# Two tiny reads of the rows that pass two loads first, and a vote moved to the end of the unfolding

## The chip, the cores and the metric

One core of one Trainium2 chip. The metric is the device time of one execution in microseconds, as the median over runs. Kernels that are compared ran on the same chip, in the same rounds.

## The reference

```python
def reference(x, w1d):            # x: (1, 384, 384, 384) bf16, w1d: (1,) bf16
    g = jnp.einsum("bhwc->bc", x) / (H * W)      # mean of each channel
    s = _sigmoid(g * w1d[0])                     # the general form has k taps, here k = 1
    return x * s[:, None, None, :]               # every row scaled by channel
```

x is 113.25 MB. It has to be read once for the sums, and it has to be scaled and written afterwards. What does not fit on the chip between the two must be read a second time.

## The kernel before

In pass one all 1152 rows of each partition are loaded and summed by TensorE. 367 of these rows stay in one big buffer, the arena; most of them packed so that four rows take the room of three (the fourth row is spread over bits of the other three that the code counts as fixed for inputs of this range). Pass two scales and stores what stayed, unpacks the packed groups, and loads the other 785 rows again, "the streamed rows". A vote says whether the bit packing was exact; if not, GpSimd would redo the kept rows at the end.

The order of all instructions is planned at build time, by a loop that imitates the DMA queue. Helpers and loop, with cuts:

```python
arena = pool.tile([P, ROWS, C], bf16, name="arena")       # 275 rows of 768 bytes per partition
...
def load(chunk, a, lo, hi):
    r0, n = chunk
    fl.add("SP", lambda: nc.sync.dma_start(out=arena[:, a : a + hi - lo, :], in_=view(xf, r0, n)[:, lo:hi, :]),
           writes=rows(a, hi - lo), dma=True)
...
def store(chunk, a, lo, hi): ...            # the reverse, arena -> out, also on SyncE's queue
def verdict(): ...                          # VectorE reduce, compare; TensorE votes; VectorE cast -> odd_i
...
while True:
    if dve_at <= now:
        ...
            can = start_pair()              # start to unpack the next group
            if can and not asked:
                verdict()
                asked = True
        ...                                 # or scale a landed chunk, or go on unpacking
    while waiting and waiting[0][0] <= now:
        _, n, then, chunk, a, lo, known = waiting.popleft()
        known.append(store(chunk, a, lo, lo + n))
    ...
    if got and todo < N_STREAM:             # free rows: load the next streamed rows
        load(STREAMED, a, todo, todo + n)
```

In this program (`LANES = 24`) every DMA on SyncE takes one of 24 completion semaphores ("lanes") in turn; a DMA whose lane is still in flight waits for it.

Of the kernel before, what the change touches and what calls it, by code (L numbers as in the profile page):

```python
# [127 lines left out]
def kernel(  # L128
# [11 lines left out]
    nc = tc.nc  # L140
# [39 lines left out]
    odd = pool.tile([P, 1], bf16, name="odd")  # L180
# [10 lines left out]
    xf = x.rearrange("b h w c -> (b h w) c")  # L191
    of = out.rearrange("b h w c -> (b h w) c")

    def view(t, r0, n):
        return t[r0 * P : (r0 + n) * P, :].rearrange("(p r) c -> p r c", r=n)

    def rows(lo, n):
        return [("a", r) for r in range(lo, lo + n)]

    fl = Flow(nc, tc)  # L200
# [6 lines left out]
    STREAMED, KEPT = (0, N_STREAM), (N_STREAM, N_KEPT)  # L207
# [154 lines left out]
    def copy_bank(i, src, dst, reads, writes):  # L362
        fl.add(
            "ACT", lambda: nc.scalar.copy(dst.bitcast(u32), src.bitcast(u32)), reads=reads, writes=writes  # L364
        )
# [56 lines left out]
    for a, n in S2 + V1 + S3 + S1 + [(U, 8), (Y, 8), (T, 5), (T + 5, 3)]:  # L422
        take_raw(a, n)
    assert summed[0] == RPP

    fl.add(
        "ACT",
        lambda: nc.scalar.activation(out=s_bf[:], in_=acc, func=ACTF.Sigmoid, scale=w_sc[:, 0:1]),  # L428
# [4 lines left out]
    def scale(a, n):  # L433
        v = arena[:, a : a + n, :]
        fl.add(
            "DVE",
            lambda: nc.vector.tensor_tensor(  # L437
                out=v, in0=v, in1=s_bf[:, None, :].to_broadcast([P, n, C]), op=Op.mult
            ),
            reads=rows(a, n) + ["s_bf"], writes=rows(a, n),  # L440
        )

    def store(chunk, a, lo, hi):
        r0, n = chunk
        return fl.add(
            "SP",
            lambda: nc.sync.dma_start(out=view(of, r0, n)[:, lo:hi, :], in_=arena[:, a : a + hi - lo, :]),
            reads=rows(a, hi - lo), dma=True,
        )
# [38 lines left out]
    def TT(n):  # L488
        return 0.15 + 0.2 * n
# [5 lines left out]
    def verdict():  # L495

        fl.add(
            "DVE",
            lambda: nc.vector.tensor_reduce(out=worst[:], in_=seen[:], op=Op.max, axis=mybir.AxisListType.X),  # L499
            reads=[("seen", k) for k in range(2 * len(pieces))], writes=["worst"],  # L500
        )
        fl.add(
            "DVE",
            lambda: nc.vector.tensor_single_scalar(out=odd[:], in_=worst[:], scalar=0.0, op=Op.is_gt),  # L504
            reads=["worst"], writes=["odd"],
        )
        fl.add(
            "PE",
            lambda: nc.tensor.matmul(votes, lhsT=ones[:], rhs=odd[:], start=True, stop=True),  # L509
            reads=["ones", "odd"], writes=["bank0"],  # L510
        )
        fl.add(
            "DVE", lambda: nc.vector.tensor_copy(out=odd_i[:], in_=votes), reads=["bank0"], writes=["odd_i"]  # L513
        )
# [44 lines left out]
    def runs():  # L559
        got, i = [], 0  # L560
        while i < ROWS:
            if idle[i]:
                j = i
                while j < ROWS and idle[j]:
                    j += 1
                got.append((j - i, i))
                i = j
            else:
                i += 1
        return got  # L570

    def send(chunk, a, lo, hi, then, known=None):

        waiting.append((dve_at, hi - lo, then, chunk, a, lo, [] if known is None else known))

    def backlog():
        return sum(e[1] for e in moves) + ROW * sum(e[1] for e in waiting)
# [9 lines left out]
    def stored(a, n):  # L587

        def f():
            for i in range(a, a + n):  # L590
                if ("a", i) in SCRATCH:
                    needed.discard(("a", i))
                else:
                    idle[i] = True
        return f
# [10 lines left out]
    line = deque((g, lo, min(2 * PIECE, QS[g] - lo)) for g in order for lo in range(0, QS[g], 2 * PIECE))  # L606
    total = sum(n for _, _, n in line)
    out_rows = 0
    turns = deque()
# [2 lines left out]
    since = None  # L612
    asked = checked = False
    stall = 0.0

    def start_pair():

        nonlocal pair, bank_at
        if not line or needed or not half[pair % 2]:
            return False  # L620
        g, lo, n = line[0]
        if g == BANKED and (bank_at is None or now < bank_at[1]):
            return False
        line.popleft()
        h = pair % 2
        at = HALVES[h]
        half[h] = False
        pair += 1
        a = bank_at[0] if g == BANKED else areas[g][0]
        a += 3 * lo  # L630
        mine = [k for k in of_group(g) if lo <= pieces[k][1] < lo + n]

        def w_done():
            nonlocal out_rows
            out_rows += n
            release(a, 3 * n)

        def u_done():
            half[h] = True

        for k in mine:
            e = pieces[k][1] - lo
            fields, three, fourth = unfold(k, a + 3 * e, at + e)
            turns.extend((fields + (None,), three + (None,), fourth + (None,)))
        f, t, _ = turns[-2]
        turns[-2] = (f, t, lambda: send(KEPT, a, c_group[g] + 3 * lo, c_group[g] + 3 * (lo + n), w_done, written))
        f, t, _ = turns[-1]
        turns[-1] = (f, t, lambda: send(KEPT, at, c_group[g] + 3 * QS[g] + lo, c_group[g] + 3 * QS[g] + lo + n, u_done, written))
        return True

    while True:

        if dve_at <= now:
            ahead = backlog()
            can = bool(turns)
            if not can and (ahead >= PENDING or not landed):
                can = start_pair()
                if can and not asked:
                    verdict()
                    asked = True  # L660
            if landed and (ahead < PENDING or not can):
                chunk, a, lo, n, end = landed.popleft()
                scale(a, n)
                dve_at = now + TT(n)
                since = (a, lo) if since is None else since
                if end or ahead < MERGE:
                    b, first = since
                    send(chunk, b, first, lo + n, stored(b, lo + n - first))
                    since = None
            elif can:  # L670
                f, t, then = turns.popleft()
                f()
                dve_at = now + t
                if then:
                    then()
        while waiting and waiting[0][0] <= now:
            _, n, then, chunk, a, lo, known = waiting.popleft()
            known.append(store(chunk, a, lo, lo + n))
            moves.append([now + LAT, n * ROW + PER_STORE, then])
        if out_rows == total and not checked and all(half):  # L680
            checked = True
            fl.add("POOL", again, reads=["odd_i", "s_bf"], writes=rows(Y, N_OVER), after=written)
        while over and over[0][0] <= now:
            over.popleft()[1]()

        got = runs()
        if bank_at is None and len(line) <= len(QS) * 2 - BANKS_AT and got and max(got)[0] >= PS:
            a = max(got)[1]
            for i in range(a, a + PS):
                idle[i] = False  # L690
            back = arena[:, a : a + PS, :].rearrange("p r c -> p (r c)")
            for i, bk in enumerate(banks):
                lo, hi = i * BANK, min((i + 1) * BANK, PS * C)
                copy_bank(i, bk[:, 0 : hi - lo], back[:, lo:hi], [("bank", i)], rows(a, PS))
            bank_at = (a, now + 5.0)
            got = runs()

        if got and todo < N_STREAM:
            n, a = max(got)
            n = min(n, CAP, N_STREAM - todo)  # L700
            ahead = backlog()
            if n >= BIG or n == N_STREAM - todo or (ahead < LOW and n >= 8) or ahead < LAST:
                load(STREAMED, a, todo, todo + n)
                for i in range(a, a + n):
                    idle[i] = False
                parts = [(STREAMED, a + e, todo + e, f - e, f == n) for e, f in split(n, PART)]
                todo += n
                moves.append([now + LAT, n * ROW + PER_LOAD, lambda parts=parts: landed.extend(parts)])

        if moves and moves[0][0] <= now:  # L710
            moves[0][1] -= DT
            if moves[0][1] <= 0:
                over.append((now + SEEN, moves.popleft()[2]))
        else:
            stall += DT
        if not (moves or waiting or over or landed or line or turns) and todo == N_STREAM:
            break
        now += DT
# [34 lines left out]
```

## Time and profile before

| | before |
|---|---|
| median of 6 runs | 722.55 us (722.34 to 722.82) |
| span of the profiled run | 721.1 us |
| moved by DMA | 303.87 MB |
| last sum ready / first scaling / first store issued | 269.7 / 270.35 / 271.33 us |
| first load of pass two issued | 282.92 us |

The prediction shows the lines that carry this. A line of a windows table has these columns: the stretch (us from the start), its length, the busy time and count of TensorE, of its weight loads, of VectorE, ScalarE and GpSimd, then TensorE's granted clock, the busy share of the 16 DMA engines, and the GB/s that they moved.

### The profile page before, as it was taken

What the parts mean: (1) busy time and instruction counts of PE and PEld (TensorE: products, weight loads), DVE (VectorE), ACT (ScalarE), POOL (GpSimd) and SP (SyncE); (2) the same over time, 40 slices, a digit from 0 to 9 for tenths busy, and PEclk for the clock granted to TensorE, in tenths of its full rate; (3) what the DMA queues carried; (4) which work ended last, traced back from release to release, by engine and by line L of the source; (5) the groups of instructions that cost most, each with busy time, mean ns of one, the idle gap of its engine ahead of it and who ended that gap; (6) DMA issues with size and microseconds to landing.
All of it is one profiled execution on the core that took longest, in us unless ns stands there. A gap on an engine that the chain in (4) does not pass through costs nothing.

```text
span 721.1 us, 3241 instructions
## 1 busy us (share of the span) xinstructions
PE 215.7 (30%) x1202; PEld 119.8 (17%) x1202; DVE 496.0 (69%) x469; ACT 115.4 (16%) x92; POOL 0.2 (0%) x4
## 2 busy tenths in 40 slices
PE   5777789888987780000000000000000000000000
PEld 2344445554543440000000000000000000000000
DVE  4600004879989809999999998999979994355330
ACT  3600003656767610001000000000000000000000
POOL 0000000000000000000000000000000000000000
PEclk9899999999999995555555555555555555555555
DMA  9999999999999978999999999999999999999997
GB/s 382 425 447 424 425 429 433 435 434 420 433 424 427 428 326 334 418 427 431 433 429 442 416 433 436 436 443 418 433 431 436 429 440 435 420 436 438 434 432 305
DMA packets 19602, 303.87 MB, mean 421 GB/s; under 512 B 2178, under 2 KB 2178, under 8 KB 6402
## 3 DMA queue, kind: packets, MB, share of 16 engines
q1 hardware_dynamic: 19584, 303.67, 98.6%
q8 instruction: 9, 0.15, 0.1%
q14 instruction: 7, 0.06, 0.0%
q10 hardware_dynamic: 2, 0.00, 0.0%
HBM read 190.41 MB, written 113.25 MB: 421 GB/s over the span
## 4 chain that ended last, share of the span: by engine, by line
DMA 53%; DVE 28%; PE 7%; another core or an unknown queue 4%; ACT 3%; SPq 0%; issue 0%; DVEq 0%
DMA arena<-in_x_dram 37%; DVE arena L437 18%; DMA out_dram<-arena 16%; PE bank L230 7%; DVE arena L254 6%; DVE arena L260 4%; ACT arena L294 3%; SPq L224 0%; ACT s_bf L428 0%; PE bank L509 0%; DVE odd L504 0%; DVE odd_i L513 0%; DVE worst L499 0%; DVEq L112 0%
## 5 line engine op out<-in xcount | busy, mean ns | idle before, releaser
L437 DVE TENSOR_TENSOR arena<-arena,s_bf 128x1536 bf16<-128x1536 bf16 (+8 forms) x102 | 241.7, 2411 | 75.5 <-DMA arena<-in_x_dram 58.2
L230 PE MATMUL bank<-arena,ones 128*128 128x384 bf16 x1152 | 207.6, 343 | 52.0 <-DMA arena<-in_x_dram 51.9
L254 DVE TENSOR_SCALAR arena<-arena 128x1536 uint16<-128x1536 uint16 (+2 forms) x247 | 145.8, 633 | 108.4 <-DMA arena<-in_x_dram 97.9
L230 PEld LDWEIGHTS bank<-arena,ones 128*128 128x128 bf16 x1152 | 114.9, 102 | 144.4 <-DMA arena<-in_x_dram 57.4
L260 DVE TENSOR_TENSOR arena<-arena 128x1536 uint16<-128x1536 uint16 (+2 forms) x114 | 121.0, 1062 | 9.7 <-PE bank L230 7.7
L294 ACT ACTIVATE arena<-arena 128x3072 uint16<-128x3072 uint16 (+1 forms) x38 | 102.5, 2696 | 142.3 <-DVE arena L254 142.3
L364 ACT COPY arena<-bank 128x512 uint32<-128x512 uint32 (+1 forms) x7 | 4.0, 570 | 70.1 <-DMA out_dram<-arena 69.9
L245 PE MATMUL bank<-ones,zeros 128*128 128x384 bf16 x48 | 8.3, 326 | 0.0
L294 ACT ACTIVATION_READ_ACCUMULATOR arena<-arena 128x1 f32 x38 | 7.1, 186 | 0.0
L245 PEld LDWEIGHTS bank<-ones,zeros 128*128 128x128 bf16 x48 | 4.7, 98 | 3.1
L509 PE MATMUL bank<-odd,ones 128*128 128x1 bf16 x1 | 0.2, 186 | 15.8 <-DVE odd L504 15.8
L364 ACT COPY bank<-arena 128x512 uint32<-128x512 uint32 (+1 forms) x7 | 3.6, 565 | 0.0
L428 ACT ACTIVATE s_bf<-bank,w_sc 128x384 bf16<-128x384 f32 x1 | 0.6, 581 | 15.9 <-PE bank L230 15.9
L509 PEld LDWEIGHTS bank<-odd,ones 128*128 128x128 bf16 x1 | 0.1, 104 | 16.2 <-DVE odd L504 16.2
L721 ACT ACT_TABLE_LOAD x1 | 1.3, 1283 | 0.7 <-PEq L737 0.7
L324 DVE TENSOR_SCALAR w_sc<-bank 128x1 f32<-128x1 f32 x1 | 0.2, 157 | 1.1 <-PE bank L319 1.1
L314 DVE MEMSET ones<- 128x128 bf16 x1 | 0.2, 165 | 1.0 <-SPq L106 1.0
L319 PE MATMUL bank<-w_bf,ones 1*128 1x1 bf16 x1 | 0.2, 179 | 2.1 <-DMA w_bf<-in_w1d_dram 2.1
L319 PEld LDWEIGHTS bank<-w_bf,ones 1*128 1x128 bf16 x1 | 0.1, 98 | 2.1 <-DMA w_bf<-in_w1d_dram 2.1
L513 DVE CAST odd_i<-bank 128x1 int32<-128x1 f32 x1 | 0.2, 159 | 0.3 <-PE bank L509 0.3
L504 DVE TENSOR_SCALAR odd<-worst 128x1 bf16<-128x1 f32 x1 | 0.2, 156 | 0.0
L499 DVE TENSOR_REDUCE worst<-seen 128x1 f32<-128x38 f32 x1 | 0.2, 180 | 0.0
(5 smaller groups left out, 0.5 us busy)
## 6 DMA issues: line engine op xcount, KB each, us to landing
arena<-in_x_dram SPq DMA_DIRECT2D x17, 4608.0 KB, 35.4
out_dram<-arena SPq DMA_DIRECT2D x6, 4608.0 KB, 43.8
arena<-in_x_dram SPq DMA_DIRECT2D x19, 1248.0 KB, 11.5
arena<-in_x_dram SPq DMA_DIRECT2D x9, 2304.0 KB, 28.3
out_dram<-arena SPq DMA_DIRECT2D x8, 2304.0 KB, 28.4
arena<-in_x_dram SPq DMA_DIRECT2D x4, 4512.0 KB, 33.6
out_dram<-arena SPq DMA_DIRECT2D x3, 4512.0 KB, 26.7
out_dram<-arena SPq DMA_DIRECT2D x9, 1248.0 KB, 11.7
```

Source lines behind the costliest of these rows:

```text
L230: return nc.tensor.matmul(acc, lhsT=ones[:], rhs=arena[:, i, :], start=first, stop=last)
L245: lambda: nc.tensor.matmul(acc, lhsT=zeros[:], rhs=ones[:, None, :].to_broadcast([P, C // P, P]), start=False, stop=False),
L254: lambda: nc.vector.tensor_scalar(out=dst, in0=src, scalar1=s0, scalar2=s1, op0=op0, op1=op1),
L260: "DVE", lambda: nc.vector.tensor_tensor(out=dst, in0=a, in1=b, op=op), reads=reads, writes=writes
L294: lambda: nc.scalar.activation(out=y, in_=y, func=ACTF.Copy, accum_out=seen[:, 2 * k + i : 2 * k + i + 1]),
L314: fl.add("DVE", lambda: nc.vector.memset(ones[:], 1.0), writes=["ones"])
L319: lambda: nc.tensor.matmul(votes, lhsT=ones[0:1, :], rhs=w_bf[0:1, 0:1], start=True, stop=True),
L364: "ACT", lambda: nc.scalar.copy(dst.bitcast(u32), src.bitcast(u32)), reads=reads, writes=writes
L428: lambda: nc.scalar.activation(out=s_bf[:], in_=acc, func=ACTF.Sigmoid, scale=w_sc[:, 0:1]),
L437: lambda: nc.vector.tensor_tensor(out=v, in0=v, in1=s_bf[:, None, :].to_broadcast([P, n, C]), op=Op.mult),
L509: lambda: nc.tensor.matmul(votes, lhsT=ones[:], rhs=odd[:], start=True, stop=True),
L721: nc.scalar.preload_act_table(ACTF.Sigmoid)
```

## The change

The intent, as far as the code tells it: read a little from the rows that the first loads of pass two will want, while the queue is otherwise idle or not full, so that these loads don't meet rows that nobody has read for a long time. As the tiny reads land in the tile `odd`, which the vote uses, the vote moves behind them.

```diff
+    def touch():
+        fl.add(
+            "SP", lambda: nc.sync.dma_start(out=odd[:], in_=view(xf, *STREAMED)[:, 0, 0:1]), writes=["odd"], dma=True,
+        )
+
+    touch()                                  # behind the last load of pass one
...
-                if can and not asked:
-                    verdict()
-                    asked = True
...
             known.append(store(chunk, a, lo, lo + n))
+            n_stored += 1
+            if n_stored == 4:
+                touch()
...
+        if not asked and not line and not turns:     # nothing left to unpack
+            verdict()
+            asked = True
```

More of the change, by code (lines that the diff above doesn't have):

```diff
@@ L614 @@
     stall = 0.0
+    n_stored = 0
     def start_pair():
```

## The prediction

> **What bounds the kernel now.** I read the page first: the header, the engine shares, the forty slices, the chain.
>
> ```profile
> span 721.1 us, 3241 instructions
> PE 215.7 (30%) x1202; PEld 119.8 (17%) x1202; DVE 496.0 (69%) x469; ACT 115.4 (16%) x92; POOL 0.2 (0%) x4
> ...
> DMA  9999999999999978999999999999999999999997
> GB/s 382 425 447 424 425 429 433 435 434 420 433 424 427 428 326 334 418 427 431 433 429 442 416 433 436 436 443 418 433 431 436 429 440 435 420 436 438 434 432 305
> ...
> HBM read 190.41 MB, written 113.25 MB: 421 GB/s over the span
> ...
> DMA 53%; DVE 28%; PE 7%; another core or an unknown queue 4%; ACT 3%; SPq 0%; issue 0%; DVEq 0%
> ```
>
> No compute engine is above 69%, and the DMA row is at 9 in every slice but two and the last. 303.66 MB at 421 GB/s is 721 us, so the time is bytes over rate. The weak slices are numbers 15 and 16 (326 and 334 GB/s, about 252 to 288 us): the change from pass one (load, sum) to pass two (scale, store, load what was not kept). The change touches only that place, so the second view is the table of windows around it, with long windows for the rest of pass two.
>
> ```profile
> 266.00:270.00 4.00, 3.63 (x22) 1.78 (x19) 0.00 (x0) 0.27 (x1) 0.00 (x0) 1.00 0.14 55
> 270.00:272.00 2.00, 0.00 (x0) 0.00 (x0) 1.66 (x2) 0.31 (x1) 0.00 (x0) 1.00 0.00 0
> 272.00:274.00 2.00, 0.00 (x0) 0.00 (x0) 2.00 (x3) 0.00 (x0) 0.00 (x0) 0.79 0.94 379
> 274.00:276.00 2.00, 0.00 (x0) 0.00 (x0) 2.00 (x2) 0.00 (x0) 0.00 (x0) 0.50 0.74 309
> 276.00:280.00 4.00, 0.00 (x0) 0.00 (x0) 4.00 (x3) 0.00 (x0) 0.00 (x0) 0.50 1.00 418
> 280.00:282.00 2.00, 0.00 (x0) 0.00 (x0) 2.00 (x1) 0.00 (x0) 0.00 (x0) 0.50 0.87 369
> 282.00:285.00 3.00, 0.00 (x0) 0.00 (x0) 3.00 (x2) 0.00 (x0) 0.00 (x0) 0.50 1.01 426
> 285.00:289.00 4.00, 0.19 (x1) 0.10 (x1) 3.65 (x10) 0.00 (x0) 0.00 (x0) 0.50 0.98 281
> 289.00:300.00 11.00, 0.00 (x0) 0.00 (x0) 10.97 (x9) 0.00 (x0) 0.00 (x0) 0.50 1.01 423
> 300.00:400.00 100.00, 0.00 (x0) 0.00 (x0) 96.65 (x89) 3.99 (x7) 0.00 (x0) 0.50 1.01 431
> ```
>
> The last two columns are DMA share and GB/s. Three losses stand here. From 266 to 272 the queue is empty: the last matmuls, the sigmoid and the first scaling stand between the last load and the first store. From 272 to 282 the stores follow VectorE, with holes of 0.12, 0.52 and 0.26 us (one minus the share, times the window). From 285 to 289 there is a third kind: the engines are busy (0.98) but move 281 GB/s. Beyond 289 the queue is full; the windows of 100 us up to 700 us all have a share of 1.00 or 1.01, though VectorE is busy 93 to 97% of the time until 600 us. So after 282 us whatever DMA time is lost or won goes one for one into the end, and VectorE time does not.
>
> What is special at 285 us? The SyncE timeline (start, duration, line, transfer) has the answer:
>
> ```profile
> 250.32 5.21 SPq L224 DMA_DIRECT2D arena<-in_x_dram  x6
> 271.33 11.54 SPq L447 DMA_DIRECT2D out_dram<-arena  x7
> 282.92 0.46 SPq L224 DMA_DIRECT2D arena<-in_x_dram  x1
> 285.21 0.33 SPq L447 DMA_DIRECT2D out_dram<-arena  x1
> ```
>
> The load issued at 282.92 is the first read of pass two, after seven stores. In the packet records the last 59 or so packets of the store ahead of it, 9984 bytes each, take 498 to 827 ns where others of that size take 375; many of its own 6144-byte packets take up to 1058 ns where 234 is usual. I summed the excess over each size's median, over 16 engines: 1.3 us for 284 to 292, and no other place after the first 5 us of the kernel reaches 0.1 us in a microsecond. Later changes from store to load show nothing like it. The loss from the rates: (426 - 281) x 4 / 426 = **1.36 us**. That is what the change can win.
>
> [...]
>
> **The change part by part.** 1. Touch one: one more transfer of 128 x 2 bytes behind the last load of pass one, issued near 255.5 us (the last of the six loads there), without a wait. It is queued behind that load, so it should run where the queue runs dry, after 266. Nobody waits for it but touch two. Cost: 0.
>
> 2. Touch two: behind the fourth store. The fourth scaling ends at 273.76 + 1.75 = 275.5, so the touch is issued at about 275.9; the fifth scaling ends at 277.2, so SyncE (0.35 to 0.46 us an issue) has time. It waits for touch one, landed some 6 us before. In the engines it is 128 / 16 = 8 data packets each. The trace has 4-byte semaphore packets of 9 ns and 2304-byte ones of 93 ns; 8 of them are 0.07 to 0.75 us. I choose 0.4 us, an estimate. The hole at 280 to 282 takes up 0.26 of it: about +0.15 us.
>
> 3. What the two buy: the first load of pass two finds its rows just read, at best -1.36 us. It is the first 8 rows of the same region, and the touch reads each partition's row 0. I give this six chances in ten: -0.82.
>
> 4. The vote on the packing ("verdict": reduce, compare, matmul, cast) moves from the start of the unfolding to its end. In the trace it takes VectorE from 285.10 to 285.83, 0.73 us. The instruction order of the new program has it last on VectorE's unfolding; the same instructions otherwise. It leaves a place where VectorE feeds a full queue: 0 us. At its new place it is still ahead of the last scalings, which wait for loads (VectorE idle 20.3 us before its last group), and the final check on GpSimd waits for stores anyway: 0 us.
>
> 5. Lanes: SyncE's completion semaphores are dealt in turns of 24, so two more transfers shift who waits for whom. In the new order only one wait is added: a store of 4992 columns near 330 us waits for touch two, landed 50 us before. 0 us.
>
> Sum: 722.55 + 0.15 - 0.82 = **721.9 us**.
>
> **Rivals.** A: the slowness belongs to the rows' addresses, and the touch cures it. For it: at 16 us into pass two it occurs once, and never again when later rows of the same region follow. Time: 722.55 - 1.36 + 0.15 = 721.3. B: it belongs to turning from stores to reads, or to something else that a tiny read does not change. For it: stores ahead of the load are stretched too. Against it: dozens of later turns are clean. Time: 722.55 + 0.15 to 0.4, so 722.7 to 723.0. C: the touch moves the stretch instead of removing it. If touch one slows the last load of pass one as the first load slowed the store ahead, the stretch lies on the path load, matmul, sigmoid, scaling, first store; up to 1.36 us come back there, and touch two may stretch the fourth store. Against it: the touch asks for 256 bytes. Time: 722.5 to 724. D: the transition itself gets shorter by more than the stretch. Nothing in the diff feeds the 6 us of empty queue at 266; I give it next to nothing.
>
> **Range and chances.** A at its best is 721.3, with a little more from VectorE's 0.73 us 720.6; C at its worst is near 724. Run-to-run spread before is 722.34 to 722.82. Eight in ten: 720.5 to 723.4. Two per cent is 14.5 us, ten times the whole stake; all of the two weak slices together is about (430 - 330) x 2 x 18 / 430 = 8.4 us. So within 2% is nearly sure.
>
> **What would show it.** Step 1: no later start of the first scaling (270.35 us before) and two small transfers into odd. Step 2: DMA share at 276 to 282 a little up, issue of the fifth store unmoved. Step 3: the rate in the first load's window back from 281 to about 420 GB/s; if it stays near 281, B; if the windows at 264 to 268 or 276 to 280 sag instead, C. Steps 4 and 5: VectorE without the 0.73 us at 285, and everything after 300 us shifted by a constant. The prediction fails if the queue runs empty somewhere in pass two, or if a wait on a lane holds SyncE for microseconds.

## The result, and the profile after

The changed kernel takes 722.76 us (median of 6 runs, 722.16 to 723.56), before 722.55. The ratio of their times is 1.0003, with a 95% interval of 0.999 to 1.0016. Ratios here are the mean time of one kernel's runs over that of the other's of the same rounds, so they are not quite the ratio of the medians.

The page of the changed kernel, header, rates and chain:

```profile
span 721.3 us, 3244 instructions
...
GB/s 382 437 434 424 427 434 428 433 433 427 426 428 427 427 322 337 418 426 428 433 432 434 425 434 432 440 432 441 416 430 439 431 438 427 430 436 440 431 430 301
...
HBM read 190.42 MB, written 113.25 MB: 421 GB/s over the span
...
DMA 57%; DVE 25%; PE 8%; another core or an unknown queue 4%; ACT 1%; SPq 1%; issue 0%; DVEq 0%
```

Slices 15 and 16 are as weak as they were (322 and 337 against 326 and 334 GB/s). SyncE's timeline has the two touches where the prediction put them:

```profile
255.64 0.43 SPq L429 DMA_DIRECT2D odd<-in_x_dram  x1
271.22 4.54 SPq L455 DMA_DIRECT2D out_dram<-arena  x4
275.80 0.46 SPq L429 DMA_DIRECT2D odd<-in_x_dram  x1
277.09 5.67 SPq L455 DMA_DIRECT2D out_dram<-arena  x3
282.81 0.46 SPq L224 DMA_DIRECT2D arena<-in_x_dram  x1
```

The first load of pass two is issued 0.1 us earlier than before, as are the stores ahead of it. The windows around it:

```profile
272.00:274.00 2.00, 0.00 (x0) 0.00 (x0) 2.00 (x3) 0.00 (x0) 0.00 (x0) 0.50 0.97 393
274.00:276.00 2.00, 0.00 (x0) 0.00 (x0) 2.00 (x2) 0.00 (x0) 0.00 (x0) 0.50 0.76 316
276.00:280.00 4.00, 0.00 (x0) 0.00 (x0) 4.00 (x3) 0.00 (x0) 0.00 (x0) 0.50 1.02 415
280.00:282.00 2.00, 0.00 (x0) 0.00 (x0) 2.00 (x1) 0.00 (x0) 0.00 (x0) 0.50 0.83 353
285.00:289.00 4.00, 0.00 (x0) 0.00 (x0) 3.96 (x8) 0.00 (x0) 0.00 (x0) 0.50 1.00 290
289.00:300.00 11.00, 0.00 (x0) 0.00 (x0) 10.78 (x9) 0.00 (x0) 0.00 (x0) 0.50 1.01 425
```

The window that the change was made for, 285 to 289 us, still moves 290 GB/s with busy engines; it was 281. No other window of the transition sags (280 to 282 us has a hole, share 0.83, as before, 0.87), so the slow stretch was neither removed nor moved. TensorE is no longer busy in it (0.19 us before): the vote has gone.

### The profile page after: what moved, and what is told of

Read it like the earlier page. It is cut to its first block, busy times and chain, and to the rows that moved or that the text cites. A ratio compares the mean times of both kernels' runs of the same rounds, so it can differ in the third digit from the quotient of the medians.

```text
span 721.3 us, 3244 instructions
## 1 busy us (share of the span) xinstructions
PE 212.9 (30%) x1202; PEld 118.5 (16%) x1202; DVE 496.5 (69%) x469; ACT 115.4 (16%) x92; POOL 0.2 (0%) x4
## 4 chain that ended last, share of the span: by engine, by line
DMA 57%; DVE 25%; PE 8%; another core or an unknown queue 4%; ACT 1%; SPq 1%; issue 0%; DVEq 0%
DMA arena<-in_x_dram 42%; DVE arena L445 17%; DMA out_dram<-arena 16%; PE bank L230 8%; DVE arena L254 5%; DVE arena L260 3%; ACT arena L294 1%; SPq L224 0%; ACT s_bf L436 0%; SPq L455 0%; SPq L760 0%; DVEq L112 0%; SPq L106 0%
## 5 line engine op out<-in xcount | busy, mean ns | idle before, releaser
L230 PE MATMUL bank<-arena,ones 128*128 128x384 bf16 x1152 | 204.7, 339 | 54.8 <-DMA arena<-in_x_dram 54.6
```

Source lines behind the costliest of these rows:

```text
L230: return nc.tensor.matmul(acc, lhsT=ones[:], rhs=arena[:, i, :], start=first, stop=last)
```

## The experiments

Twelve kernels ran, all correct. "Excess" below is time of data packets over the median of their size, per engine, summed from the packet records around the first load of pass two; it is 1.3 us both before and after the change. The clean places of the kernel before stay under 0.1 us in any one microsecond.

**1. The parts of the change.** The vote alone (the diff without `touch`):

> The kernel before with only the vote moved to the end of the unfolding, no touch. If VectorE time behind 282 us is worth nothing (my step 4): ratio 0.999 to 1.001, though VectorE starts the unfolding about 0.8 us earlier (285.1 instead of 285.9). Rival: the 0.8 us of VectorE is worth its full length, 721.7 us, ratio 0.999; or the moved vote costs, and the touches had gained what it lost: over 1.001.

722.34 us, ratio 1.0000 (0.9987 to 1.0014). VectorE's chain is 0.8 us ahead at 285 us, and at the end nothing of it is left: behind 282 us, where the queue is full (share 1.00 or 1.01 in the windows of 100 us up to 700 us), 0.8 us of VectorE time was worth nothing. The rival of a gain of its full length, ratio 0.999, is not excluded by the interval, but the trace shows none of it: the span is 721.2 us.

The touches alone, vote as before. They need a tile of their own:

```diff
     odd = pool.tile([P, 1], bf16, name="odd")
+    peek = pool.tile([P, 1], bf16, name="peek")     # touches write this
     arena = pool.tile([P, ROWS, C], bf16, name="arena")
```

> The kernel before plus the two touches (into a tile of their own, 2 bytes per partition); the vote stays where it was. Theory B (the slow stretch at the first load of pass two does not belong to rows gone cold; each touch costs about 0.1 us of queue): ratio to before 0.999 to 1.001, rate in 285 to 289 us near 285 GB/s as in both kernels. Theory A (the touch cures the stretch, and the change lost the gain elsewhere, by the moved vote): rate there above 380 GB/s and some 1.3 us faster, 0.998.

729.86 us, ratio 1.0103 (1.0088 to 1.0119). Neither theory had this. The trace was slower from the first 100 us on, long before any touch, so the touches could not be the cause. The built program shows what else the edit did: the arena starts at byte 16928 of each partition, not at 16896: the 2-byte tile moved it by 32 bytes. Two runs separate shift and touches: the same kernel with `peek` allocated behind all other tiles, and the kernel before with a 32-byte tile ahead of the arena and no touch.

> The same as the run of the touches alone, but the 2-byte tile is allocated behind all others, so the big buffer starts on the same address as in the kernel before (16896[...]) and not 32 bytes later. If the 7 us of that run came from the shift of the buffer: ratio 0.999 to 1.001. If they came from the touches with the vote left early: about 1.010 again.

> The kernel before with a 32-byte tile ahead of the big buffer (it starts at 16928) and nothing else but the one memset of that tile. If the shift is the cause: 729.5 to 730 us, ratio 1.010, with the queue's rate some 1 per cent lower in pass one as well. Rival (touches): 1.000.

Touches without shift: 722.79 us, ratio 1.0003 (0.999 to 1.0017). Shift without touches: 730.16 us, ratio 1.0104 (1.0088 to 1.0119). So the 7 us were the shift, and the touches alone do nothing that these runs resolve, as the whole change does nothing: the stretch stands in their trace too (264 GB/s at 285 to 289 us, 1.39 us of excess), and a gain of 1.36 us (ratio 0.998) is outside the interval. Two windows of 100 us of the shifted kernel, one in each pass:

```profile
100.00:200.00 100.00, 87.26 (x510) 50.37 (x508) 69.09 (x94) 52.59 (x37) 0.00 (x0) 0.97 1.01 428
300.00:400.00 100.00, 0.00 (x0) 0.00 (x0) 95.09 (x86) 4.00 (x7) 0.00 (x0) 0.50 1.01 428
```

The kernel before has 430 and 431 there. The queue is as busy and carries less, by 0.5 and 0.7% in these windows; 1% was expected. The rest of the 7 us was not traced, and the tiles behind the arena moved with it, so that the arena's start alone does it is argued from the queue's rate. The whole shift costs 1.0% of the time here. How 32 bytes bring the rate down was not shown.

**2. The price of a touch.** Two touches ahead of each store from the 11th on, 92 in all, each into a column of its own, with 72 lanes so that no wait on a lane comes in.

> Two touches ahead of each store from the 11th on, 92 in all, each into a column of its own, with 72 completion lanes so that no lane is waited for; the queue is full all that time. Cost of one touch by itself. If the packet records (9 ns for each of 8 packets and a semaphore packet per engine, 0.08 us) are its whole cost: +7 us, ratio 1.010. If a tiny read holds the queue for more (0.3 us each): +28 us, 1.04. If it is free: 1.000.

727.65 us against 722.59, ratio 1.0073 (1.0057 to 1.0088). 5.06 us over 92 is **0.055 us a touch** in a full queue, less than the packet records made me expect (0.08). Whatever SyncE and the 72 lanes cost is within these 5.06 us. At that price the two touches of the change come to 0.11 us, less than the spread of the runs (722.34 to 722.82 us before).

**3. Is it the rows?** If rows not read for 250 us were slow, rows read just before should not be. Pass two reads the streamed rows from the end:

```diff
-                load(STREAMED, a, todo, todo + n)
+                r0 = N_STREAM - todo - n
+                load(STREAMED, a, r0, r0 + n)
```

> The kernel before, but pass two reads the streamed rows from the last to the first, so its first load takes rows that were read only some 20 to 60 us before. If the stretch at the first load belongs to rows not read for 250 us: the rate in 285 to 289 us rises from 281 to about 420 GB/s and the time falls by 1.3 us (ratio 0.998). If it belongs to the first read behind a run of stores, whatever the address: rate still near 285 GB/s, ratio 0.9995 to 1.0005.

722.52 us, ratio 1.0001 (0.9987 to 1.0015). The window of the stretch in this kernel:

```profile
285.00:289.00 4.00, 0.18 (x1) 0.10 (x1) 3.65 (x9) 0.00 (x0) 0.00 (x0) 0.50 0.99 281
```

281 GB/s, the same as before, on rows read only 20 to 60 us earlier. And the other way round, all later loads of pass two take rows that were not read since pass one, and none of them is slow (in the kernel before, no microsecond from 289 us on has more than 0.07 us of excess). The age of the rows is not the cause, so a touch can't help by making them fresh.

**4. Which read is it?** One more real read between stores 4 and 5, of 8 rows or of 1, into rows already stored.

```diff
+            n_stored += 1
+            if n_stored == 4:
+                load(STREAMED, Y, 0, 8)          # second kernel: 0, 1
```

> The kernel before plus one real read between stores 4 and 5: 8 rows of 768 bytes per partition, the same rows as the first load, into rows already stored (thrown away later). 1.85 us of queue, about 0.8 of it in the holes up to 282 us. If the stretch belongs to the first sizeable read behind the idle gap and the stores, whichever it is: it appears at 277 to 281 us, the rate at 285 to 289 us rises to about 420 GB/s, ratio about 1.000 to 1.001. If it belongs to the load at 282.9 itself (its place, its length of queue ahead): rate there still near 285 GB/s, ratio 1.0015 to 1.003.

> The same with 1 row of 768 bytes per partition (0.23 us of queue). If any real read takes the stretch on itself, the rate at 285 to 289 us rises and part of the 1.36 us falls in the holes: ratio 0.998 to 0.9995. If a read must fill the queue to be hit (the touch of 2 bytes was not): rate at 285 to 289 still near 285 GB/s, ratio 1.000.

With 8 rows: 724.35 us, ratio 1.0025 (1.001 to 1.0041). The time alone would fit the other theory (1.0015 to 1.003), as the added 1.85 us found less room in the holes than I thought; the windows decide:

```profile
276.00:280.00 4.00, 0.00 (x0) 0.00 (x0) 4.00 (x3) 0.00 (x0) 0.00 (x0) 0.50 1.04 326
280.00:282.00 2.00, 0.00 (x0) 0.00 (x0) 2.00 (x1) 0.00 (x0) 0.00 (x0) 0.50 0.92 341
282.00:285.00 3.00, 0.00 (x0) 0.00 (x0) 2.96 (x4) 0.00 (x0) 0.00 (x0) 0.50 1.04 438
285.00:289.00 4.00, 0.18 (x1) 0.10 (x1) 3.69 (x8) 0.00 (x0) 0.00 (x0) 0.50 1.00 425
```

The stretch has moved to the new read (326 GB/s at 276 to 280 us, 1.26 us of excess at 277 to 281), and the load at 283.8 us is clean: 425 GB/s. So the stretch belongs to the first read of some size among the stores, whichever it is. (The early read takes the rows of the first load; alone, this run would also fit rows that it had freshened, but experiment 3 rules that out.) With 1 row: 722.96 us, ratio 1.0005 (0.9991 to 1.0018); the small read takes 0.18 us of excess, and the first load keeps its stretch (306 GB/s). The read of 768 bytes per partition did not take it over, nor did the touch of 2 bytes after the change (290 GB/s at 285 to 289 us).

**5. Why only the first?** Later loads also follow runs of stores and are clean (in the kernel before, the load near 437 us follows six stores). The packet records gave an idea. Up to the stretch a DMA of 1.83 us of data (6144 bytes per partition at 430 GB/s) runs from its first to its last packet in 1.99 us; the 16 engines go side by side (their first packets behind the empty queue start within 0.13 us, from 272.18 us on). A few transfers behind the stretch, one of 2.97 us of data takes 3.8 us. The idea, called lockstep: after the empty queue of 266 to 272 us the engines start together, and all turn from writes to reads in the same moment; later they have drifted apart, and the turn of one lies beside the work of others. The rival is a cost paid once in pass two, however the engines stand. First test: part the engines by cutting stores 5 and 6 unevenly (partitions 0 to 63, 64 to 71, 72 to 79, 80 to 127), with even cuts of 32 partitions as the control.

> The kernel before, but stores 5 and 6 are cut by partitions into 64, 8, 8 and 48. If the 8-partition pieces go to half of the engines alone, that half carries 9 packets and the other 7 of each store, so the 16 engines come to the first load some 1.2 us apart (2 x 0.23 + 2 x 0.375). Theory, lockstep: the stretch arises because all 16 engines turn from writes to reads in the same moment, and later turns are clean because the engines have drifted apart. Then the excess of packet time falls from 1.3 us per engine to under 0.9 and the rate at 285 to 289 us rises above 310 GB/s; ratio 0.999 to 1.0005. Rival, a cost paid once for the first read in pass two, however the engines stand: rate still near 285 GB/s, excess still 1.2 to 1.4 us.

> Control of the uneven cuts: the same two stores cut into four equal pieces of 32 partitions[...]. Both theories: rate at 285 to 289 us near 285 GB/s, excess near 1.3 us, ratio 0.9995 to 1.001.

As tests of the time both failed. 726.68 us, ratio 1.0053 (1.0039 to 1.0067), and 725.90 us, ratio 1.0039 (1.0024 to 1.0055): the cuts themselves are slow. The control, at its cut stores:

```profile
276.00:280.00 4.00, 0.00 (x0) 0.00 (x0) 4.00 (x3) 0.00 (x0) 0.00 (x0) 0.50 1.03 333
280.00:282.00 2.00, 0.00 (x0) 0.00 (x0) 2.00 (x1) 0.00 (x0) 0.00 (x0) 0.50 0.96 277
```

In the uneven kernel, 32 packets of 6144 bytes in a row, from 278.5 us on, take about 475 ns where 234 is usual; why was not shown. So the time of these kernels can't be compared with the kernel before, but the stretch can. By their completion packets, the 16 engines of the uneven kernel end the last cut piece between 286.2 and 288.4 us, two microseconds apart (0.15 us apart at the end of the same store before). The microsecond from 288 us is clean (0.03 us of excess). Then the first load comes:

```profile
288.00:289.00 1.00, 0.00 (x0) 0.00 (x0) 0.97 (x3) 0.00 (x0) 0.00 (x0) 0.50 0.97 399
289.00:293.00 4.00, 0.00 (x0) 0.00 (x0) 4.00 (x4) 0.00 (x0) 0.00 (x0) 0.50 1.04 287
```

287 GB/s, and 1.43 us of excess from 289 to 293 us (1.38 in the control, from 288 to 293): what the rival expected, four microseconds later. Engines that lay this far apart still paid in full. That speaks against lockstep, though the slow cut stores just ahead leave the test unclean.

Second test: bring the engines into step again, later. Store 29, near 407 us, waits until everything has landed; three more stores follow, then a load.

```diff
+            drained = fl.queued["SP"][-24:] if n_stored == 29 else ()
-            known.append(store(chunk, a, lo, lo + n))
+            known.append(store(chunk, a, lo, lo + n, drained))   # added to what it waits for
```

> The kernel before, but store 29 (21,504 bytes per partition, near 407 us) waits until everything issued has landed; three more stores, then a load follow. The drain leaves the queue empty for about 3 us and puts the 16 engines back in step. Lockstep: the stores after it run with the engines together, and a stretch of 0.7 to 1.3 us of packet excess shows at the load that follows (near 430 to 445 us), where the kernel before has under 0.1; ratio 1.005 to 1.008. Rival, paid once: no stretch there; ratio 1.003 to 1.006.

728.01 us, ratio 1.0075 (1.006 to 1.0091), inside what lockstep expected; the interval touches the rival's 1.006, so the trace has to decide. The kernel before, then the drained one:

```profile
416.00:420.00 4.00, 0.00 (x0) 0.00 (x0) 4.00 (x2) 0.00 (x0) 0.00 (x0) 0.50 1.00 432
436.00:440.00 4.00, 0.00 (x0) 0.00 (x0) 4.00 (x3) 0.00 (x0) 0.00 (x0) 0.50 1.02 442
448.00:452.00 4.00, 0.00 (x0) 0.00 (x0) 2.43 (x1) 0.00 (x0) 0.00 (x0) 0.50 0.97 415
```

```profile
416.00:420.00 4.00, 0.00 (x0) 0.00 (x0) 3.96 (x3) 0.00 (x0) 0.00 (x0) 0.50 0.71 297
436.00:440.00 4.00, 0.00 (x0) 0.00 (x0) 3.97 (x4) 0.00 (x0) 0.00 (x0) 0.50 1.01 344
448.00:452.00 4.00, 0.00 (x0) 0.00 (x0) 0.72 (x1) 0.00 (x0) 0.00 (x0) 0.50 0.96 332
```

The empty queue stands at 416 to 420 us (share 0.71). The first load behind it comes to the engines at 438 us, and there the stretch is again: engines busy (1.01), 344 GB/s, 0.81 us of packet excess in the three microseconds from 436, where the kernel before has none to speak of. A second one stands where that load ends: in the microsecond from 448 us exactly 16 packets, as many as there are engines, take some 2.1 us instead of 1.36. So it is not paid once per pass. It came back after the queue had run empty. The drain was to do two things at once, empty the queue and bring the engines into step (whether they were in step behind it was not measured), so it doesn't say which of them matters.

Third test, from the other side: part the engines with a read for 8 partitions alone (16 rows, thrown away) between stores 6 and 7.

> The kernel before plus one read for 8 partitions alone (16 rows of 768 bytes each, thrown away) between stores 6 and 7, when the queue has just filled. If its 8 packets go to half of the engines, that half falls behind by 0.5 us (12,288 bytes at the usual rate)[...]. Lockstep: the engines no longer turn to the first load together, so the excess there falls from 1.3 us per engine to under 0.9 and the rate in the four microseconds of the stretch is above 320 GB/s instead of 281; ratio 0.9990 to 1.0010, as the added packets cost about what is won. Rival, or if a small partial read does not part the engines: excess 1.2 us or more, rate under 300 GB/s, ratio 1.0005 to 1.002.

723.69 us, ratio 1.0012 (0.9999 to 1.0026). The windows:

```profile
282.00:285.00 3.00, 0.00 (x0) 0.00 (x0) 2.96 (x4) 0.00 (x0) 0.00 (x0) 0.50 0.97 326
285.00:289.00 4.00, 0.19 (x1) 0.10 (x1) 3.26 (x8) 0.00 (x0) 0.00 (x0) 0.50 1.01 335
```

The rate at the first load is 335 instead of 281 GB/s, as lockstep expected, and the excess from 285 to 290 us is 0.97 us instead of 1.3, just short of what it expected. But 0.60 us of excess now stands at 282 to 285 us, around the added read, and in sum nothing is won. The packet records fit another reading at least as well, a cost that an engine pays mostly at its own first read behind the gap. In the store ahead of the added read, the eight engines that read have two slow packets each (420 to 773 ns instead of 375), the other eight one (467 to 540 ns). In the store ahead of the first load it is the other eight whose last two packets are slow (740 to 780 ns); those that have read before are clean there. (The records don't name a packet's engine; it is inferred from start and end times.) So this run does not show lockstep, and the uneven kernel speaks against it. What the runs show is when the cost comes: at the first read of some size behind an emptied queue (281 GB/s over 4 us at the start of pass two, 344 behind the drain). How it arises stays open.

No version beat the kernels: the stretch can be moved, at its full price, or split, at the same price.

## Why the prediction was right or wrong

The time was right: 721.9 us predicted, 722.76 measured, within 720.5 to 723.4, and "within 2%" holds. But the gain of 0.65 us that it forecast did not come. By its steps:

1. *Touch one costs nothing.* Right. Its packets start between 265.03 and 268.38 us, as the queue runs dry; the first scaling starts at 270.23 us, 0.12 us earlier than before, and nobody waits for the touch.
2. *Touch two, 0.4 us, of which 0.15 remain.* The place was right, the size seven times too large: 0.055 us in a full queue (92 touches, +5.06 us). I had overlooked a packet here: the trace before holds a data packet of 2 bytes, the load of `w1d` at 1.8 us, and it takes 7 ns, which points to the low end of the prediction's 0.07 to 0.75 us. The 256 packets of the touches take 9 ns each in the trace after. The fifth store is issued at 277.09 us (277.20 before), not held up by the touch.
3. *The touches cure the slow stretch, six chances in ten, -0.82 us.* This is the step that failed. The location and the stake (1.36 us) were right, the cause was not: the rate there is 290 GB/s after the change, and 281 in the run whose first load takes rows read 20 to 60 us before. I had read "once, at the first load" as "rows that have gone cold", though the packets of the store ahead, which reads none of these rows, spoke against it: 40 of them are slow (not 59, as I wrote), and they carry 0.83 of the 1.29 us. In its place the runs showed a cost of the first sizeable read behind an empty queue; rival B, with 722.7 us, was what came.
4. *The moved vote is worth 0.* Right: ratio 1.0000 alone.
5. *Lanes, 0.* Right: the touches alone, with the same shift of lanes, give 1.0003.

Rival C, that a touch would take the stretch to itself, was wrong for 2 bytes, right for 8 rows: there it moved. The range held because it was built on the stake, not because the guess was good: at most 1.4 us of 722 hung on it.

## What to carry to other kernels

A transfer that is slow at one place in a trace has an address, a neighbour and a moment; before paying for a cure, change the address alone (read the rows in another order) and see whether the slowness stays. When an experiment needs one more tile, allocate it behind the buffers that the DMA queue works on: a control of 2 bytes moved a buffer by 32 and cost more than everything under test (730.16 against 722.72 us for the shift alone). And where the queue is the bound, keep it from running empty: besides the gap, these runs paid at the first read behind it (1.3 us of packet time at the start of pass two, 0.8 us behind the drain).
